# Batch 1 of a retention layer in two-pair blocks with DMA transposes, at the end of the first token tile

## Chip, cores, metric

The kernel runs on one core of a Trainium2 chip. The metric is the time of one execution on the device, in microseconds (us). The kernel before took 535.51 us (median of 4 runs, 535.12 to 537.06; the prediction starts from one of them, 535.76).

The engines are named as the profile names them: PE multiplies matrices, PEld loads its weights, DVE is the vector engine, ACT the scalar engine, POOL the general engine, SP the engine that only starts transfers. DMA queue q1 ("hardware") carries what SP starts, q0 ("software") what POOL starts.

## The reference

```
# retention, batch 8, heads 8, 576 tokens, 64 per head
scores = (1/8) * q @ k.T                       # per batch and head
ret    = (scores * D) @ v                      # D[i,j] = gamma_h ** (i-j) for i >= j, else 0
x      = ret.transpose(0, 2, 1, 3).reshape(4608, 512)
# four experts, mixed by given probabilities
p      = domain_probs / (domain_probs.sum(-1) + 1e-9)
out    = sum over e of p[:, e] * (relu(x @ w1[e]) @ w2[e])     # w1 512x1024, w2 1024x512
```

## The kernel before

Retention is computed in chunks of 128 tokens. The decay is split into factors on q and k, so a chunk needs scores (k against q), a causal mask, key-value products that are summed from chunk to chunk, and values. The 576 tokens of a batch are four chunks and a remainder of 64. The experts run over nine tiles of 512 tokens. In tile 0 ("plain": up and down projections of the four experts, in 32 numbered slots), the retention of batch 1 has to be slipped in between the projections; later batches are slipped into later tiles.

Scores need q and k with the head dimension on partitions, so both are transposed after their cast to bf16. There are two ways to do this. Both are in the class "Unit" (256 tokens of four heads), which serves batches 0 and 1:

```python
        def trans_pe(self, between=0):                      # 8 PE instructions, one ACT copy
            self.qk = atp.tile([128, 2, 2, 2, C], BF16, tag="qkT", name="qkT0")
            pt = ring_tile("pt", [128, 2, 2, 2, 2 * C], BF16)
            for i, n in ((1, "k"), (0, "q")):
                # ...
                        nc.tensor.transpose(pt[:, i, r, g, 0:C], # ... bf of n ...
                                            ident)
            nc.scalar.activation(# ... self.qk <- pt ...
                                 Copy)

        def trans_dma(self):                                # two transfers on SP's queue, no PE
            self.qk = atp.tile([128, 2, 2, 2, C], BF16, tag="qkT", name="qkT1")
            for i, n in ((1, "k"), (0, "q")):
                nc.sync.dma_start_transpose(out=self.qk[:, i].rearrange("p r g t -> p (r g) t"),
                                            in_=self.bf(n).rearrange("p r h d -> p (r h d)"))
```

Batch 1 is four units in tile 0. The first two are transposed on PE, the last two by DMA:

```python
    load_w2(0); load_w1(1); later_tables(); load_w2(1); load_rem(0, nc.gpsimd)   # POOL's queue, q0
    load_w1(2); load_w2(2); load_v(0); load_v(1); load_w1(3); load_v(2); load_w2(3)
    # ...
    def v_cast(u):
        vs[u].cast("k", nc.vector)
        vs[u].cast("q", nc.vector)
        vs[u].cast("v", nc.scalar)
        if u > 1:
            vs[u].trans_dma()
        if u == 0:
            load_v(3)
    # slots of cast, PE transpose, scores and key-values, values
    for u, (c, tr, sc, o) in enumerate(((17, 20, 22, 23), (19, 22, 24, 25), (24, 0, 28, 29), (25, 0, 29, 30))):
        add(c, lambda u=u: v_cast(u))
        if u < 2:
            add(tr, lambda u=u: vs[u].trans_pe())
        add(o, lambda u=u: vs[u].values())
        add(sc, lambda u=u: v_head(u))
```

Batches 2 to 7 use the class "Duo": two pairs of heads over all 512 tokens, in one "block" (values of the block before, key-values, scores), always with DMA transposes on SP's queue:

```python
        def cast(self, p):                    # casts of k, q (and a copy of v), then
            # ...
            for t, n in ((self.kT[p], "k"), (self.qT[p], "q")):
                nc.sync.dma_start_transpose(out=t, in_=bfs[p % 2][n][:, :, :, :].rearrange("p c h d -> p (c h d)"))
```

Of the kernel before, what the change touches and what calls it, by code (L numbers as in the profile page):

```python
# [23 lines left out]
def kernel(  # L24
# [10 lines left out]
    nc = tc.nc  # L35
# [79 lines left out]
    def load_unit(raw, b, hf, g, eng):  # L115
        for n, src in srcs:
            eng.dma_start(out=raw[n],
                          in_=src[b, 4 * g:4 * g + 4, 2 * C * hf:2 * C * hf + 2 * C, :]
                          .rearrange("h (p r) d -> p h (r d)", r=2))

    units0 = ((0, 0), (1, 0), (0, 1), (1, 1))
    p0 = const.tile([128, NT // 128, E], FP32, name="p0")
    prb = tpool.tile([128, N // 128, E], FP32, tag="p1", name="prb")
    for u, (hf, g) in enumerate(units0):
        load_unit({n: raw0[u][n][:, :, :, :].rearrange("p h r d -> p h (r d)") for n in "kqv"}, 0, hf, g, nc.sync)
    nc.sync.dma_start(out=p0, in_=moe_domain_probs[0:NT, :].rearrange("(g p) e -> p g e", p=128))
    nc.sync.dma_start(out=prb, in_=moe_domain_probs.rearrange("(p t) e -> p t e", p=128))
# [103 lines left out]
    class Duo:  # L231
        def __init__(self, b, d):
            self.b, self.d = b, d
            self.ps = slice(2 * d, 2 * d + 2)
            self.qT, self.kT, self.sT = {}, {}, {}

        def cast(self, p):
            for n, eng, g in (("k", nc.gpsimd, gk), ("q", nc.gpsimd, gq)):
                eng.tensor_tensor(bfs[p % 2][n], raw1[n],  # L239
                                  g[:, :, 2 * p:2 * p + 2].unsqueeze(3).to_broadcast([128, NC, 2, D]), op=MULT)  # L240
            nc.gpsimd.tensor_copy(bv[p], raw1["v"])
            self.kT[p] = dpl.tile([128, NC, C], BF16, tag="kT", name="kT", bufs=2)
            self.qT[p] = dpl.tile([128, NC, C], BF16, tag="qT", name="qT", bufs=4)
            for t, n in ((self.kT[p], "k"), (self.qT[p], "q")):
                nc.sync.dma_start_transpose(out=t, in_=bfs[p % 2][n][:, :, :, :].rearrange("p c h d -> p (c h d)"))
# [4 lines left out]
        def kv(self):  # L250
            kvp = ring_tile("kvp", [128, 2, NC, D])
            for i, p in self.pairs():
                for c in range(NC):
                    for j in range(2):
                        nc.tensor.matmul(kvp[64 * j:64 * j + 64, i, c:NC, :], lhsT=bfs[p % 2]["k"][:, c, j, :],
# [19 lines left out]
        def values(self):  # L275
            o = ring_tile("o", [128, 2, SM])
            for i, p in self.pairs():
# [3 lines left out]
            for i, p in self.pairs():  # L281
                for c in range(NC):
                    for j in range(2):
                        nc.tensor.matmul(o[64 * j:64 * j + 64, i, c * C:(c + 1) * C], lhsT=bv[p][:, c, j, :],  # L284
                                         rhs=self.sT[p][:, j, c, :], start=False, stop=(c == NC - 1),
                                         skip_group_check=True)
            n0 = self.b * S
            a = 0
            while a < SM:
                t = (n0 + a) // NT  # L290
                z = min(SM, (t + 1) * NT - n0)
                nc.scalar.activation(xt_of(t)[:, self.ps, n0 + a - t * NT:n0 + z - t * NT], o[:, :, a:z], Copy)  # L292
                a = z

# [58 lines left out]
    def up_group(h, t, e, i):  # L353
        ph = ring_tile("ph", [128, 2, NT])
        x = xt_of(t)
        for f in range(2):
            fc = 2 * i + f
            for dc in range(NDC):
                nc.tensor.matmul(ph[:, f, :], lhsT=w1_sb[e][:, dc, fc * 128:(fc + 1) * 128],  # L359
                                 rhs=x[:, dc, :], start=(dc == 0), stop=(dc == NDC - 1))  # L360
        fk = e * NFC + 2 * i
# [50 lines left out]
    def w_sum(which, lo, hi):  # L412
        sl = slice(lo, hi)
        if which == 3:
            nc.vector.tensor_tensor(t3w[:, sl], wx[1][:, sl, 1], wx[0][:, sl, 1], op=SUB)
        if which == 1:
            nc.vector.tensor_tensor(wx[0][:, sl, 1], wx[0][:, sl, 1], wx[0][:, sl, 0], op=SUB)
        if which == 2:
            nc.vector.tensor_tensor(t2w[:, sl], wx[1][:, sl, 1], wx[0][:, sl, 1], op=SUB)
        if which == 4:  # L420
            nc.vector.tensor_tensor(t4w[:, sl], wx[1][:, sl, 0], t2w[:, sl], op=SUB)
# [88 lines left out]
    class Unit:  # L510
        def __init__(self, b, hf, g, raw, bf, carry=None):
            self.b, self.hf, self.g, self.raw, self.bfs, self.carry = b, hf, g, raw, bf, carry
# [5 lines left out]
        def cast(self, n, engine):  # L518
            dst = self.bf(n).rearrange("p r h d -> p h r d")
            if n == "v":  # L520
                if engine is nc.scalar:
                    nc.scalar.activation(dst, self.raw["v"], Copy)
                else:
                    engine.tensor_copy(dst, self.raw["v"])
# [16 lines left out]

        def trans_dma(self):
            self.qk = atp.tile([128, 2, 2, 2, C], BF16, tag="qkT", name="qkT1")
            for i, n in ((1, "k"), (0, "q")):
                nc.sync.dma_start_transpose(out=self.qk[:, i].rearrange("p r g t -> p (r g) t"),
                                            in_=self.bf(n).rearrange("p r h d -> p (r h d)"))
# [20 lines left out]
        def kv(self):  # L567
# [14 lines left out]
            if hf == 1 and self.carry is None:  # L582
# [7 lines left out]
            for j in range(2):  # L590
                jr = slice(64 * j, 64 * j + 64)
                dst = sbd[jr, gs, 2 * hf:2 * hf + 2, jr]
                src = kvp[jr, :, :, jr]
                if hf == 1 and self.carry is not None:
                    nc.vector.tensor_tensor(dst, src,
                                            self.carry[jr, gs, :].unsqueeze(2).to_broadcast([64, 2, 2, D]), op=ADD)
                else:
                    nc.scalar.activation(dst, src, Copy)
                if hf == 0 and self.carry is not None:
                    nc.vector.tensor_copy(self.carry[jr, gs, :], kvp[jr, :, 1, jr])  # L600

        def values(self):
            self.values_own()
            self.values_carried()
# [12 lines left out]
        def values_carried(self):  # L617
# [9 lines left out]
            n0 = self.b * S + i0  # L627
            for g in range(2):
                p = 2 * self.g + g
                a = 0  # L630
                while a < 2:
                    t = (n0 + C * a) // NT
                    z = 2 if n0 + 2 * C <= (t + 1) * NT else a + 1
                    lo, hi = n0 + C * a - t * NT, n0 + C * z - t * NT
                    w = z - a
                    nat = lambda ap: ap.rearrange("p (a t r) -> p a r t", a=w, r=2)
                    src = lambda x, y: o[:, x:y, g, 0:C].rearrange("p a (r t) -> p a r t", r=2)
                    if hi <= NT:
                        nc.scalar.activation(nat(xt_of(t)[:, p, lo:hi]), src(a, z), Copy)
                    else:  # L640
                        m = (NT - lo) // 2
                        for tt, d0, u0, u1 in ((t, lo, 0, m), (t + 1, 0, m, C // 2)):
                            nc.scalar.activation(
                                xt_of(tt)[:, p, d0:d0 + 2 * (u1 - u0)].rearrange("p (t r) -> p r t", r=2),
                                o[:, a, g, 0:C].rearrange("p (r t) -> p r t", r=2)[:, :, u0:u1], Copy)
                    a = z

    bfv0 = lambda g: {(n, hf): bf0[n][:, hf, g] for n in "kqv" for hf in range(2)}
    us = [Unit(0, hf, g, raw0[u], bfv0(g)) for u, (hf, g) in enumerate(units0)]
# [35 lines left out]
    mixing_weights()  # L685
# [8 lines left out]
    first = ctx.enter_context(ExitStack())  # L694
    fpool = first.enter_context(tc.tile_pool(name="fpool", bufs=1))
    q1 = fpool.tile([128, 2, 2, 4, D], BF16, name="q1")
    raw2 = fpool.tile([128, 3, 2 * NC * D], FP32, name="raw2")
    raw1u = {n: raw1[n][:, :, :, :].rearrange("p c j d -> p (c j d)") for n in "kqv"}
    bf1 = [{}, {}]
    for g in range(2):  # L700
        kv1 = opool.tile([128, 2, 2, 4, D], BF16, tag="o", name=f"kv1_{g}")
        for n in "kqv":
            a = bfs[g][n][:, :, :, :].rearrange("p c j d -> p (c j d)").rearrange("p (r h d) -> p r h d", r=2, h=4)
            bf1[g][n, 0] = a
            bf1[g][n, 1] = q1[:, g] if n == "q" else kv1[:, "kv".index(n)]
    rx = [spool.tile([128, 1024], FP32, tag="S", name=f"rx{i}") for i in range(2)]
    rawxu = {"k": rx[0][:, 0:512], "q": rx[0][:, 512:1024], "v": rx[1][:, 0:512]}
    raws = (raw1u, rawxu, {n: raw2[:, "kqv".index(n), :] for n in "kqv"}, raw1u)
    carry = tpool.tile([128, NP, D], FP32, tag="p1", name="carry")
    vs = [Unit(1, hf, g, {n: raws[2 * hf + g][n].rearrange("p (h r d) -> p h r d", h=4, r=2) for n in "kqv"},  # L710
               bf1[g], carry) for hf in range(2) for g in range(2)]

    def load_v(u):
        load_unit({n: raws[u][n].rearrange("p (h x) -> p h x", h=4) for n in "kqv"}, 1, vs[u].hf, vs[u].g, nc.gpsimd)

    load_w2(0)
    load_w1(1)
    later_tables()
# [4 lines left out]
    load_v(0)  # L723
    load_v(1)
    load_w1(3)
    load_v(2)
    load_w2(3)

    def remainder(slots, b, at):
        add = lambda i, f: slots.setdefault(i, []).append(f)  # L730
        x = Rem(b)
        l, c, tr, s, o = at
        if b > 0:
            add(l, lambda: load_rem(b))
        add(c, lambda: x.cast(nc.vector))
        add(tr, x.trans_pe)
# [137 lines left out]
```

## Time and profile before

| | before |
|---|---|
| time | 535.51 us (4 runs) |
| span of the profiled run | 533.7 us |
| PE | 526.5 us busy, 4260 instructions |
| PE's waits | under 3 us in all |
| granted PE clock | full in every slice |

The lines behind this table are in the prediction below. Two more views follow, the second behind the prediction. The first is the table of stretches. Columns: the stretch, its length, busy time and count of PE, PEld, DVE, ACT and POOL, then the granted PE clock, the mean busy share of a DMA engine, and GB/s. Before:

```profile
60.00:70.00 10.00, 10.00 (x123) 5.16 (x122) 8.19 (x14) 6.20 (x12) 0.00 (x0) 1.00 0.64 150
70.00:80.00 10.00, 9.98 (x102) 4.87 (x101) 5.97 (x10) 3.87 (x11) 0.00 (x0) 1.00 0.55 150
```

The second is the view of the DMA queues from 69 to 75 us, when the kernel before runs its only DMA transposes of tile 0 (queue: packets, MB, share of 16 engines; then transfers with their size or count and the median us from issue to landing):

```profile
q1 hardware_dynamic: 1984, 0.48, 39.9%
...
qkT<-kv SPq DMA_TRANSPOSE x2, 2.5
qkT<-q SPq DMA_TRANSPOSE x2, 3.2
```

No line of q0 stands there: the software queue, with the weights and the loads of batch 1, was empty. These are medians of two: the four transposes landed 2.4 to 4.0 us after their issue under that condition.

### The profile page before, as it was taken

Reading aid. Unit: us, or ns where it says so; the run is one execution under the profiler, and the core shown is the slowest. Engines: PE = TensorE matmul, PEld = TensorE weight load, DVE = VectorE, ACT = ScalarE, POOL = GpSimd, SP = SyncE. Lnnn points to the kernel's source line nnn. Section 1 sums busy time; section 2 is a strip of 40 time slices with the busy share of each in tenths; the row PEclk is TensorE's granted clock in tenths of the full one; section 3 lists DMA queues with packets and bytes.
Section 4 is the critical chain, followed back from the end, with each engine's and each line's share of the span. In section 5 each row is a group of like instructions: output and inputs, shape, how many; then the busy total and the mean of one; then the engine's idle time right before and its main releaser. Section 6 shows DMA issues by size and latency. Waiting matters only on the chain.

```text
span 533.7 us, 10229 instructions
## 1 busy us (share of the span) xinstructions
PE 526.5 (99%) x4260; PEld 342.4 (64%) x4260; DVE 361.7 (68%) x456; ACT 86.0 (16%) x175; POOL 144.5 (27%) x187
## 2 busy tenths in 40 slices
PE   8999999999999999999999999999999999999997
PEld 4644544478745885478646865587548844884486
DVE  6426668895577767697578767777765567557763
ACT  4723450012101121020101001100110000000010
POOL 5734104236235334335132603153000000000000
PEclk9999999999999999999999999999999999999999
DMA  9999947877879967937353655454010111110001
GB/s 240 205 213 250 239 114 190 165 156 168 143 168 166 174 138 145 158 81 167 101 135 95 152 134 112 107 120 124 20 41 21 60 39 41 41 41 20 1 21 60
DMA packets 145118, 63.55 MB, mean 119 GB/s; under 512 B 124240, under 2 KB 135888, under 8 KB 145072
## 3 DMA queue, kind: packets, MB, share of 16 engines
q1 hardware_dynamic: 134752, 43.50, 38.2%
q0 software_dynamic: 10176, 19.27, 16.4%
q8 instruction: 33, 0.54, 0.4%
q10 hardware_dynamic: 144, 0.13, 0.1%
q14 instruction: 13, 0.11, 0.1%
HBM read 53.56 MB, written 9.51 MB: 118 GB/s over the span
## 4 chain that ended last, share of the span: by engine, by line
PE 73%; ACT 2%; DVE 0%; issue 0%
PE ph L359 37%; PE pd L471 34%; ACT xt L292 2%; PE o L284 1%; PE o L279 1%; PE py L471 1%; DVE h L365 0%; PE sr L338 0%; PE or L344 0%; PE or L346 0%; DVE ob L499 0%
## 5 line engine op out<-in xcount | busy, mean ns | idle before, releaser
L359 PE MATMUL ph<-xt,w 128*128 128x512 bf16 x1136 | 251.0, 379 | 0.8 <-DVE h L365 0.2
L365 DVE SCALAR_TENSOR_TENSOR h<-ph,pB 128x1024 bf16<-128x1024 f32 x128 | 156.5, 1224 | 58.7 <-PE ph L359 58.0
L359 PEld LDWEIGHTS <-w 128*128 128x128 bf16 x1136 | 109.9, 98 | 127.9
L471 PEld LDWEIGHTS <-h 128*128 128x128 bf16 x1024 | 100.0, 98 | 13.3
L471 PEld LDWEIGHTS <-s 128*128 128x128 bf16 x768 | 75.0, 98 | 8.7
L471 PE MATMUL pd<-wx,h 128*128 128x256 bf16 x512 | 61.1, 273 | 0.2
L471 PE MATMUL pd<-wx,s 128*128 128x256 bf16 x512 | 61.1, 273 | 0.0
L220 POOL DMA_DIRECT2D pB<-pd x28 | 15.8, 565 | 150.9 <-DVE h L365 131.8
L506 POOL TENSOR_TENSOR ob<-v,p 128x256 f32<-128x256 f32 x15 | 11.3, 755 | 114.0 <-DVE v L503 92.5
L239 POOL TENSOR_TENSOR bf_k<-raw_k,gk 128x512 bf16<-128x512 f32 x24 | 25.8, 1073 | 35.3 <-DMA raw_k<-in_k_dram 17.4
L271 DVE TENSOR_TENSOR sT<-s,tri 128x1024 bf16<-128x1024 f32 x24 | 28.3, 1219 | 6.4 <-PE s L269 6.4
L292 ACT ACTIVATE xt<-o 128x768 bf16<-128x768 f32 (+6 forms) x24 | 13.0, 594 | 116.8 <-PE o L284 116.8
L444 DVE TENSOR_TENSOR s<-s,h 128x1024 bf16<-128x1024 bf16 x32 | 31.2, 1013 | 0.0
L471 PE MATMUL pd<-t4w,h 128*128 128x256 bf16 x256 | 30.6, 273 | 0.0
L394 PE MATMUL po<-wx,h 128*128 128x512 bf16 x128 | 29.1, 379 | 0.1
L471 PE MATMUL pd<-t3w,h 128*128 128x256 bf16 x240 | 28.7, 273 | 0.0
L471 PE MATMUL pd<-t2w,s 128*128 128x256 bf16 x240 | 28.6, 273 | 0.0
L479 ACT ACTIVATE p<-pd 128x256 f32<-128x256 f32 x16 | 6.1, 384 | 138.8 <-PE pd L471 106.2
L239 POOL TENSOR_TENSOR bf_q<-raw_q,gq 128x512 bf16<-128x512 f32 x24 | 26.9, 1120 | 3.3 <-DMA raw_q<-in_q_dram 3.1
L442 DVE TENSOR_TENSOR s<-h 128x1024 bf16<-128x1024 bf16 x32 | 24.8, 816 | 0.0
L448 DVE TENSOR_TENSOR s<-h,s 128x1024 bf16<-128x1024 bf16 x32 | 24.7, 811 | 0.0
L488 DVE TENSOR_TENSOR u<-pd,p 128x256 f32<-128x256 f32 x15 | 6.4, 425 | 22.5 <-PE pd L471 22.5
(158 smaller groups left out, 375.2 us busy)
## 6 DMA issues: line engine op xcount, KB each, us to landing
pB<-pd POOLq DMA_DIRECT2D x28, 256.0 KB, 3.7
raw_k<-in_k_dram SPq DMA_DIRECT2D x48, 128.0 KB, 2.8
raw_q<-in_q_dram SPq DMA_DIRECT2D x48, 128.0 KB, 3.0
raw_v<-in_v_dram SPq DMA_DIRECT2D x48, 128.0 KB, 3.0
wx<-in_moe_w_dram POOLq DMA_DIRECT2D x4, 1024.0 KB, 15.4
out_dram<-oa SPq DMA_DIRECT2D x16, 256.0 KB, 2.2
out_dram<-ob SPq DMA_DIRECT2D x15, 256.0 KB, 2.2
w<-in_moe_w_dram POOLq DMA_DIRECT2D x3, 1024.0 KB, 15.1
```

Source lines behind the costliest of these rows:

```text
L220: eng.dma_start(out=pB[t, e], in_=pd[e:e + 1, t * NT:(t + 1) * NT].to_broadcast([128, NT]))
L239: eng.tensor_tensor(bfs[p % 2][n], raw1[n], g[:, :, 2 * p:2 * p + 2].unsqueeze(3).to_broadcast([128, NC, 2, D]), op=MULT)
L271: nc.vector.tensor_tensor(sT[:, :, :, :].rearrange("p j c t -> p (j c) t"), s[:, :, :, :].rearrange("p j c t -> p (j c) t"), tri[:, :].uns ...
L292: nc.scalar.activation(xt_of(t)[:, self.ps, n0 + a - t * NT:n0 + z - t * NT], o[:, :, a:z], Copy)
L359: nc.tensor.matmul(ph[:, f, :], lhsT=w1_sb[e][:, dc, fc * 128:(fc + 1) * 128], rhs=x[:, dc, :], start=(dc == 0), stop=(dc == NDC - 1))
L365: nc.vector.scalar_tensor_tensor(h[:, fk:fk + 2, :], ph, 0.0, pB[t, e][:, :].unsqueeze(1).to_broadcast([128, 2, NT]), op0=MAX, op1=MULT)
L394: nc.tensor.matmul(po[:, g, :], lhsT=h[:, e * NFC + fc, ns * 128:(ns + 1) * 128], rhs=wx[e // 2][:, (e % 2) * NFC + fc, :, :].rearrange("p ...
L442: nc.vector.tensor_tensor(self.alloc("s1")[:, l], h[:, l, self.b], h[:, r, self.b], op=ADD)
L444: nc.vector.tensor_tensor(self.alloc("s2")[:, l], self.s1[:, l], h[:, l, self.a], op=SUB)
L448: nc.vector.tensor_tensor(self.alloc("s4")[:, l], h[:, r, self.a], self.s2[:, l], op=SUB)
L471: mm = nc.tensor.matmul(dst, lhsT=src[:, kk, tok], rhs=rhs(c), start=(start and c == 0), stop=(c == KH - 1), skip_group_check=True)
L506: nc.gpsimd.tensor_tensor(self.ob[:, HF:Dm], self.v, self.p5, op=ADD)
```

## The change

The intent is to take work off PE in tile 0. Batch 1 becomes two blocks like those of the later batches, with all transposes by DMA, and the remainder of batch 0 is transposed by DMA too. Batch 0's units go in another order (tokens 0 to 255 first), and the probabilities are loaded behind the first down weights. The values v of batch 1 are cast to bf16 by their load. One weight-sum step in four goes from DVE to POOL. Cut to its core:

```diff
-    units0 = ((0, 0), (1, 0), (0, 1), (1, 1))
+    units0 = ((0, 0), (0, 1), (1, 0), (1, 1))
-    nc.sync.dma_start(out=p0, ...)            # and prb
     load_w2(0)
+    nc.gpsimd.dma_start(out=p0, ...)
     load_w1(1)
+    nc.gpsimd.dma_start(out=prb, ...)
     later_tables()
     load_w2(1)
     load_rem(0, nc.gpsimd)
     load_w1(2)
     load_w2(2)
-    load_v(0)
-    load_v(1)
     load_w1(3)
-    load_v(2)
+    load_first(0)                              # pairs of heads, runs of 256 bytes; v cast in the load
+    load_first(1)
     load_w2(3)
+    load_first(2)
 ...
-    remainder(slots, 0, (-1, 13, 15, 16, 17))
-    # ... v_cast, v_head and the slots of the four units
+    for at, f in ((10, lambda: rem0.cast(nc.vector)), (10, rem0.trans_dma), (24, rem0.scores), (25, rem0.values)):
+        add(at, f)
+    add(11, lambda: load_first(3))
+    for p, at in enumerate((21, 23, 27, 28)):
+        add(at, lambda p=p: firsts[p // 2].cast(p, nc.vector))    # with the DMA transposes of pair p
+    add(27, lambda: block(firsts[0], None))
+    add(29, firsts[0].values)
+    add(31, lambda: block(firsts[1], None))
+    add(27, lambda: [load_p(1, e, nc.gpsimd) for e in range(E)])
 ...
-    for j, ats in enumerate(((18, 18, 19, 20), (20, 21, 23, 23), (28, 28, 29, 29), (30, 30, 40, 41))):
+    for j, ats in enumerate(((17, 17, 18, 18), (20, 20, 21, 22), (28, 30, 36, 40), (28, 28, 29, 29))):
+        eng = nc.gpsimd if j == 3 else nc.vector
 ...
+        if t == 1:                             # values of the second block between halves of up groups
+            up_part(1, 0, 0, (0, 1))
+            up_part(1, 0, 1, (0, 1))
+            firsts[1].values(True)
+            up_part(1, 0, 2, (0, 1))
```

## The prediction

> **What bounds the kernel now.** I read first the page's busy shares and its 40 slices, then the view of who waited for whom on the matrix engine (PE), then the timeline of PE, and last the timelines of the engines that feed it.
>
> ```profile
> PE 526.5 (99%) x4260; PEld 342.4 (64%) x4260; DVE 361.7 (68%) x456; ACT 86.0 (16%) x175; POOL 144.5 (27%) x187
> ...
> PE   8999999999999999999999999999999999999997
> ...
> PEclk9999999999999999999999999999999999999999
> DMA  9999947877879967937353655454010111110001
> ```
>
> PE is busy 526.5 of 533.7 us, in every slice, at full clock. So time falls only if PE instructions go, and it rises if the new order makes PE wait. The waits of PE are these, in total:
>
> ```profile
> PE w L138 <- DVE zz L131: 1.3, 1, 1.3
> PE s L560 <- ACT qkT L539: 0.5, 2, 0.3
> PE o L623 <- ACT sbd L598: 0.5, 2, 0.2
> PE pt L537 <- DVE bf_q L526: 0.2, 1, 0.2
> PE o L623 <- DVE sbd L595: 0.2, 1, 0.2
> PE ph L359 <- DVE h L365: 0.2, 1, 0.2
> ```
>
> Columns: total us, times, longest. Under 3 us, half of it before the first instruction. There is no stall for the change to remove; the prize must be PE work. The PE timeline has both forms of it side by side: batch 1 as four small "units" inside tile 0 (lines 537, 560, 578, 613, 623), and batch 2 already as two-pair blocks (lines 255, 269, 279, 284):
>
> ```profile
> 56.20 0.39 PE L537 MATMUL pt<-ident,bf_k 128*128 128x128 bf16 x4
> 56.42 0.39 PE L537 MATMUL pt<-ident,bf_q 128*128 128x128 bf16 x4
> 56.64 3.62 PE L394 MATMUL po<-wx,h 128*128 128x512 bf16 x16
> 60.19 0.42 PE L560 MATMUL s<-qkT 64*64 64x128 bf16 x16
> 60.54 0.72 PE L578 MATMUL kvp<-bf_v,bf_k 128*128 128x128 bf16 x8
> 61.19 0.40 PE L537 MATMUL pt<-ident,bf_k 128*128 128x128 bf16 x4
> ...
> 125.32 0.50 PE L279 MATMUL o<-qT,sbd 128*128 128x128 bf16 x6
> 125.75 0.64 PE L284 MATMUL o<-sT,bf_v 128*64 128x128 bf16 x16
> 126.22 0.72 PE L255 MATMUL kvp<-v,bf_k 128*64 128x256 bf16 x16
> 126.88 0.62 PE L269 MATMUL s<-qT,kT 64*128 64x128 bf16 x16
> 127.62 1.91 PE L471 MATMUL pd<-wx,h 128*128 128x256 bf16 x16
> ```
>
> First number: start; second: duration with the pipeline's tail. What a piece costs PE is the distance from its start to the next piece's start: 60.19 to 61.19 is 1.00 us for one unit's scores and key-value products.
>
> **What the Trainium skill says.** "TensorE: Matmul & The Clock Gate", part 1, section "Wait — 56ns, not 53.3ns?", gives 215.7 ns from start to start for 512 columns at the warm clock. The trace agrees: 16 matmuls of 128x512 between 22.27 and 25.7 us are 3.45 us, 216 ns each; the 379 ns of the groups is a latency that overlaps. "SBUF — State Buffer", section "Who interferes with whom", says that a VectorE (DVE) instruction with two SBUF inputs contends with a GpSimd (POOL) instruction that reads SBUF, the second waiting for the first's end. The trace agrees: a weight sum on DVE takes 0.69 us as a rule, and 2.16 us at 100.80 us, while POOL multiplies at 100.80 to 101.86. "DMA: Bandwidth & Descriptors", Specifications, gives 512 B as the least transfer for line rate. The trace agrees in kind: batch 1's second unit landed about 2.1 us after its first (0.75 MB in 512-byte runs), while the remainder's 0.38 MB in 256-byte runs took some 1.9 us of the same queue. "GPSIMD Engine Reference", section "Instruction dispatch", gives about 2.5 cycles per element for two inputs on POOL; 512 elements in 1.04 us are 2.4 cycles at that page's 1.2 GHz.
>
> **The change, part by part.**
>
> Removed from PE, start to start from the timeline: the remainder's transposes 0.54 (46.66 to 47.20); two units' transposes 0.44 + 0.46; four units' scores and key-value products 1.00 + 1.01 + 1.00 + 1.09; four units' values 0.47 + 0.47 + 0.68 + 0.94. Sum 8.10 us, 196 instructions.
>
> Added to PE: two blocks. Batch 2's blocks stand 1.45, 1.40 and 1.39 us for key-values and scores, and 0.90 and 1.00 us for values. Two blocks cost 2 x (1.40 + 0.95) = 4.70 us, 108 instructions. The built programs confirm the count: 88 matmuls fewer. **PE saves 8.10 - 4.70 = 3.40 us.**
>
> Batch 0's order: the same instructions, the 12-product key-value step moved from the second unit to the third. The end of that stage hangs on the fourth unit: its queries are awaited for 0.2 us by DVE at 13.5 us, then follow transpose, copy, scores, mask and values to about 20.6 us, where the second half of the up projection can begin. Order does not move the fourth load, so I count 0, plus or minus 0.3. The first half's tokens are ready earlier, but nobody waited for them.
>
> Probabilities: two loads leave the front of the first queue and go behind the first down weights, which landed at about 26.0 us (POOL, which waits for them, resumes at 26.09) against PE's first use at 25.95. The 16 matmuls before it need 3.45 us and have 3.68. So some 0.2 us is lost there now; an earlier landing saves at most that. **-0.2 us.**
>
> Loads of batch 1: four pairs in 256-byte runs, in place of four units in 512-byte runs. My estimate from the two rates above is 3.6 us a pair in place of 2.3, hence the last pair lands some 5 us later: the DMA share falls to 0.05 at 66 us now, so at about 71 then. Weights gain: the last up weights go ahead of batch 1, and the last down weights wait behind 1.5 MB and not 2.25. They are needed 4.4 us sooner (about 68 us, as this much of the removed work lies before), so this is even.
>
> The end of tile 0 is where a new wait can arise. Call T0 the end of the first block, about 69.5 us (now the last up group of tile 0 ends at 72.53; less 4.4, plus 1.4). Pair 2's transposes may start when the first block's scores have read the two key buffers. The queue's own timeline shows 1.2 to 1.3 us per transpose issued, and 2.5 to 2.9 us to landing. DVE has in a row: two masks (2.35 us for a pair at 109.51), the two casts of pair 3 (0.69 each), a weight sum, two evictions (1.41), another sum, two evictions, two masks. Pair 3's casts thus end at T0 + 3.8, its transposes land at T0 + 7.5. PE reaches the second block after four down groups (1.73 each) and one values step: T0 + 7.9. Without disturbance it just fits. Then the score buffer waits for the eviction (about T0 + 7.3), the first split up group for the second (T0 + 9.9 against T0 + 9.3), and the split up groups (1.73 us) cover the two masks. So 0.5 us of stall at best.
>
> POOL disturbs it: four weight sums of 1024 elements, about 2.1 us each at the 2.4 cycles, are in program order right behind the last loads, so they run from about 71 to 79 us, beside DVE's casts and sums with two SBUF inputs. If two or three of those wait about 1 us each, the second block starts 1 to 3 us late, part of which the slack eats. **My central stall is 1.3 us.** The remainder of batch 1 is similar: its loads sit behind the first output in the queue, transposes land at about 90, and PE wants them at 90.8. I count 0 to 1 us, inside the stall.
>
> Later tiles keep their instructions, and just shift. Sum: -3.4 - 0.2 + 1.3 = -2.3 us, on 535.76: **533.4 us.**
>
> **Rivals.** (1) The tail of tile 0 becomes a wait: loads, casts, transposes and masks no longer keep up, and PE stands 4 us or more; the time is 535.5 to 537. For it: pair 3 has no slack in my count, DVE is 9.1 of 10 us busy at 80 to 90 now, and the POOL contention hits just there. Against it: four groups of independent matmuls and the split up groups were put there to cover. (2) Full hiding: POOL's sums fall in gaps, the transposes come in time, and everything counted on PE is won, also a few tenths in the first 26 us: 531.5 to 532.2. For it: PE has had every other wait hidden so far. (3) The loads: if DMA runs in 256-byte pieces cost more than I estimate, the last down weights come after 69.5 us and pair 3 after 74, and PE loses 2 to 5 us: 535 to 538. Against it: the DMA share shows a valley after 66 us that takes up 5 us.
>
> **Range and chances.** The saving on PE is counted and certain to perhaps 0.3 us; the stall is 0.3 to 5 us. That gives 531.4 to 536.2, with the middle nearer the low end. A gain of 2% would need 10.7 us, three times all the PE work removed; a loss of 2% would need a stall of 14 us. Faster 0.02, within 2% 0.96, slower 0.02.
>
> **What would show each step.** PE at 4172 instructions and about 3.4 us less busy; the two new blocks at 1.4 and 0.95 us. In the PE waits a new row for the second block (scores behind DVE or a transpose) or for values behind the mask, together 1 to 2 us between 65 and 95 us. On POOL four sums of about 2.1 us near 71 to 79 us; on DVE casts or sums above 0.69 us in the same stretch. The last pair lands at 70 to 73 us. The first down group starts about 3.5 us after the up group before it. A PE wait over 3 us, at the last down weights or the second block, proves me wrong; so would a start stage that moved by over 0.5 us.

## The result and the profile after

The changed kernel took **544.04 us** (median of 4 runs, 541.57 to 544.64) against 535.51 us. The ratio is 1.0145, with a 95% interval of 1.0107 to 1.0183: 1.4% slower, inside the 2% band, and 7.8 us above the upper end of my range. Ratios here and below are the mean time of one kernel's runs over that of the other's of the same rounds, so they are not quite the ratio of the medians quoted.

The page of the changed kernel, busy totals and the 40 slices of 13.5 us:

```profile
PE 524.8 (97%) x4172; PEld 341.0 (63%) x4172; DVE 359.0 (66%) x444; ACT 80.7 (15%) x157; POOL 167.4 (31%) x209
...
PE   8999929999999999999999999999999999999997
...
PEclk9999979999999999999999999999999999999999
DMA  9999998768667768556546593534110111010001
```

The 88 instructions are gone, but slice 6 (67.7 to 81.3 us) has PE at 2 tenths and its clock at 7. The DMA row says that this slice is the last of a long stretch of nearly full DMA engines (six slices at 9). PE's waits have a new first line, and its timeline shows the place (start, duration, instruction, in brackets the idle time just before and what ended it):

```profile
PE s L269 <- DMA qT<-bf_q: 9.8, 2, 6.3
```

```profile
67.73 0.75 PE L255 MATMUL kvp<-bf_v,bf_k 128*64 128x256 bf16 x16
71.98 0.40 PE L269 MATMUL s<-qT,kT 64*128 64x128 bf16 x8 [3.50 <-DMA qT<-bf_q]
78.70 0.61 PE L269 MATMUL s<-qT,kT 64*128 64x128 bf16 x8 [6.32 <-DMA qT<-bf_q]
79.25 5.70 PE L414 MATMUL po<-wx,h 128*128 128x512 bf16 x16
...
85.79 3.63 PE L414 MATMUL po<-wx,h 128*128 128x512 bf16 x16
```

The scores of the first block waited for the transposed queries of pair 0 (3.50 us) and then of pair 1 (6.32 us). Two equal groups of 16 down-projection matmuls follow: the first took 5.70 us, the second 3.63 us. The stretches show why (columns as before):

```profile
60.00:70.00 10.00, 8.48 (x63) 4.12 (x61) 3.87 (x7) 5.44 (x7) 6.23 (x9) 1.00 1.34 108
70.00:80.00 10.00, 1.70 (x18) 0.91 (x19) 3.17 (x4) 0.00 (x0) 4.60 (x7) 0.66 1.33 184
```

The granted clock (third from last) has a mean of 0.66 over the second stretch. That is a mixture. Cut at the places where it changes, the stretches read:

```profile
69.00:73.20 4.20, 0.40 (x8) 0.25 (x8) 0.00 (x0) 0.93 (x2) 0.00 (x0) 1.00 1.05 153
73.30:83.40 10.10, 4.70 (x18) 1.87 (x19) 6.57 (x7) 0.00 (x0) 7.93 (x10) 0.50 1.43 196
83.50:90.00 6.50, 6.50 (x61) 3.47 (x59) 3.35 (x5) 1.08 (x2) 6.26 (x4) 1.00 0.89 241
```

PE was busy for 0.40 of 4.20 us, and then the clock was half for about 10 us, in which the first group ran.

The sum closes. Waits 3.50 + 6.32 = 9.8 us, slow matmuls 5.70 - 3.63 = 2.1 us, less the 3.4 us that the change saves on PE: +8.5 us. The spans differ by 541.9 - 533.7 = 8.2 us.

Next, why the transposes came so late. SP's timeline shows their issue:

```profile
59.15 1.19 SPq L245 DMA_TRANSPOSE kT<-bf_k  x1
60.43 1.23 SPq L245 DMA_TRANSPOSE qT<-bf_q  x1
62.99 1.67 SPq L245 DMA_TRANSPOSE kT<-bf_k  x1
64.76 2.21 SPq L245 DMA_TRANSPOSE qT<-bf_q  x1
```

The queries of pair 0 were issued at 60.43 and released PE at 71.98; those of pair 1 went out at 64.76 and released it at 78.70. The casts and the issue were in time; from issue to the release of PE it took 11.6 and 13.9 us, where the kernel before shows about 3 to landing. The DMA view gives the medians over 58 to 68 us, and the queues' packets over 71 to 76 us:

```profile
kT<-bf_k SPq DMA_TRANSPOSE x2, 8.9
qT<-bf_q SPq DMA_TRANSPOSE x2, 12.6
```

Each line is a median of two. One by one, the keys and queries of pair 0 landed 3.5 and 11.4 us after issue, those of pair 1 14.3 and 13.8.

```profile
q0 software_dynamic: 736, 0.77, 88.9%
q1 hardware_dynamic: 746, 0.18, 41.1%
```

The two queues had almost the same number of packets through in those 5 us. A transpose of 128 x 512 bf16 elements is 131,072 bytes, and 0.18 MB in 746 packets is about 240 bytes each, so one transpose is some 512 packets of 256 bytes (worked out from these lines). The software queue's packets were about 1 KB each. If the DMA engines serve the queues in turn, packet by packet, each small packet of a transpose waits for a large packet of a load. The Trainium skill has such turns: "DMA: Bandwidth & Descriptors", section "Queues, rings and completion order", says that each DMA engine goes round the queue rows it has work for, and drains one whole packet before it moves on. Its packet is a bundle of several descriptors (single pieces of a transfer); no run here shows that this is what the profile counts as a packet. The equal counts agree with turns, one for one. I had not drawn on the page in the prediction.

The fast one of the four fits too. From 60 to 62 us, when the keys of pair 0 were on their way, the packets of the software queue were small themselves, about 140 bytes:

```profile
q0 software_dynamic: 1054, 0.15, 134.3%
q1 hardware_dynamic: 538, 0.13, 33.1%
```

So small packets beside small ones got through in 3.5 us.

The equal counts hold from 67 to 77 us, but for 69 to 70 us (27 and 18, when both nearly stood): single microseconds read 139 and 135, 151 and 147, 107 and 108, 211 and 215. They do not hold everywhere. From 62 to 67 us both queues crawled, the hardware queue more (6 to 47 packets in a microsecond, the software queue 59 to 95). Taking turns is thus not the whole of it, and this crawl stays unexplained.

The remainder's transposes met the same fate earlier: issued at 37.93 and 39.46, landed 11.6 and 12.1 us later, with 625 and 624 packets in the two queues from 40 to 46 us. Nobody waited for them, but in that stretch, by the same reading, they took turns from the weights.

### The profile page after: what moved, and what is told of

Same layout as the page of the kernel before. It is cut to its first block, busy times and chain, and to the rows that moved or that the text cites. A ratio compares the mean times of both kernels' runs of the same rounds, so it can differ in the third digit from the quotient of the medians. Undisturbed runs are those within 1.5% of the kernel's fastest.

```text
span 541.9 us, 10073 instructions
## 1 busy us (share of the span) xinstructions
PE 524.8 (97%) x4172; PEld 341.0 (63%) x4172; DVE 359.0 (66%) x444; ACT 80.7 (15%) x157; POOL 167.4 (31%) x209
## 4 chain that ended last, share of the span: by engine, by line
PE 72%; ACT 2%; DVE 0%; issue 0%
PE ph L375 36%; PE pd L491 33%; ACT xt L302 2%; PE o L285 1%; PE o L280 1%; PE py L491 1%; DVE h L385 0%; PE or L356 0%; PE sr L350 0%; PE or L358 0%; PE s L269 0%; PE kvp L255 0%; DVE ob L519 0%
## 5 line engine op out<-in xcount | busy, mean ns | idle before, releaser
L491 PEld LDWEIGHTS <-h 128*128 128x128 bf16 x1024 | 100.0, 98 | 13.3
L218 POOL DMA_DIRECT2D pB<-pd x32 | 17.9, 566 | 155.6 <-DVE h L385 148.7
L271 DVE TENSOR_TENSOR sT<-s,tri 128x1024 bf16<-128x1024 f32 x28 | 33.0, 1218 | 6.7 <-PE s L269 6.7
L302 ACT ACTIVATE xt<-o 128x768 bf16<-128x768 f32 (+8 forms) x30 | 15.3, 567 | 134.9 <-PE o L285 134.9
L414 PE MATMUL po<-wx,h 128*128 128x512 bf16 x128 | 30.5, 399 | 0.0
L414 PEld LDWEIGHTS <-h 128*128 128x128 bf16 x128 | 12.6, 102 | 16.7 <-issue 2.9
```

The costliest lines, as they stand in the source:

```text
L218: eng.dma_start(out=pB[t, e], in_=pd[e:e + 1, t * NT:(t + 1) * NT].to_broadcast([128, NT]))
L271: nc.vector.tensor_tensor(sT[:, :, :, :].rearrange("p j c t -> p (j c) t"), s[:, :, :, :].rearrange("p j c t -> p (j c) t"), tri[:, :].uns ...
L302: done.append(nc.scalar.activation(xt_of(t)[:, 2 * self.d + i:2 * self.d + z2, n0 + a - t * NT:n0 + z - t * NT], o[:, i:z2, a:z], Copy))
L414: nc.tensor.matmul(po[:, g, :], lhsT=h[:, e * NFC + fc, ns * 128:(ns + 1) * 128], rhs=wx[e // 2][:, (e % 2) * NFC + fc, :, :].rearrange("p ...
L491: mm = nc.tensor.matmul(dst, lhsT=src[:, kk, tok], rhs=rhs(c), start=(start and c == 0), stop=(c == KH - 1), skip_group_check=True)
```

## The experiments

The theory: **a DMA transpose issued while the software queue is busy with large packets can land 9 to 18 us after its issue, and not 2.5 to 3; the first block's scores wait for it, and the clock falls during the wait.** (Not each one does: besides the 3.5 us above, those of pairs 2 and 3 in the changed kernel landed after 4.6 to 5.5 us beside a busy queue.) In the texts, A is this theory. Its rivals, where named, are the slower loads, the POOL sums beside DVE, and the other parts of the change (order, probabilities). Each kernel was timed over 3 rounds (the two so marked over 5), with the kernel before on the same chip. All outputs are right.

| run | made from | median us | ratio to before [95%] |
|---|---|---|---|
| before_units_dma | before | 544.03 | 1.0146 [1.0125, 1.0168] |
| before_front | before | 535.21 | 0.9992 [0.9972, 1.0012] |
| after_pairs_pe | after | 537.56 | 1.0029 [1.0006, 1.0051] |
| after_rem_pe | after | 541.46 | 1.0100 [1.0081, 1.0119] |
| after_both_pe | after | 538.35 | 1.0035 [1.0008, 1.0062] |
| after_dve_sums | after | 542.02 | 1.0125 [1.0106, 1.0144] |
| pairs_pe_late_p | after | 539.76 | 1.0085 [1.0035, 1.0134] |
| pairs_pe_dve | after | 538.84 | 1.0058 [1.0036, 1.0080] |
| all_pairs_pe | after | 535.42 | 0.9984 [0.9939, 1.0030] |
| all_pairs_pe_dve (5 rounds) | after | 534.82 | 0.9982 [0.9966, 0.9998] |
| all_pe_dve (5 rounds) | after | 533.93 | 0.9976 [0.9961, 0.9992] |
| after_filled | after | 546.91 | 1.0202 [1.0164, 1.0241] |
| before_idle_transposes | before | 536.81 | 1.0019 [0.9999, 1.0040] |
| before_idle_copies | before | 535.95 | 1.0007 [0.9991, 1.0022] |

### One part of the change alone, in the kernel before

**DMA transposes for the first two units.** Loads, order, blocks and sums stay as before.

```diff
-        if u > 1:
-            vs[u].trans_dma()
+        vs[u].trans_dma()
 ...
-        if u < 2:
-            add(tr, lambda u=u: vs[u].trans_pe())
```

> The kernel before with one thing changed: the first two units of batch 1 get their transposes from the DMA queue (as units 3 and 4 already do) at the moment of their casts, 50 to 54 us, while the software queue still loads weights. Theory A (transposes issued beside the software queue's loads crawl, packet by packet in turn with them): the four transposes land 9 to 14 us after issue and not 2.5, PE waits 1 to 5 us in all at the scores of these units, the last down weights land later; PE saves 0.9 us; time 536 to 540. Theory B (the loads of batch 1 in 256-byte runs and with a cast in the DMA are what is slow; here they stay in 512-byte runs): the transposes land in 2.5 to 4 us, no new PE wait, time 534.6.

It took 544.03 us, the same loss as the whole change, from this part alone. The loss is larger than the text expected; the direction is A's, and nothing else of the change is needed for it. PE's waits:

```profile
PE s L560 <- DMA qkT<-bf_q: 4.5, 1, 4.5
```

The four transposes landed 10.6, 12.4, 16.8 and 14.9 us after issue. The clock fell here too (a mean of 0.68 from 60 to 66 us).

**The front alone**: batch 0's order and the later probabilities (cut; the steps that work out the mixing weights move to other slots with them).

```diff
-    units0 = ((0, 0), (1, 0), (0, 1), (1, 1))
+    units0 = ((0, 0), (0, 1), (1, 0), (1, 1))
-    (loads of p0 and prb on nc.sync)
     load_w2(0)
+    nc.gpsimd.dma_start(out=p0, ...)
     load_w1(1)
+    nc.gpsimd.dma_start(out=prb, ...)
```

> The kernel before with only the two small parts of the change: batch 0's units in the new order and the probabilities behind the first down weights (batch 1 and all transposes as before). My reckoning: nothing waits on either, 0 to 0.3 us of gain; time 535.2 to 535.8, no PE wait above 0.5 us that the kernel before does not have. If one of these parts were the cause of the loss, 537 or more.

535.21 us: no effect on the time, as expected.

### Transposes back on PE, in the changed kernel

**Pairs 0 and 1** (the first block):

```diff
+            if self.b == 1 and p in PE_PAIRS:     # PE_PAIRS = (0, 1)
+                return                            # no DMA transposes
...
+        def trans_pe(self, p):                    # 8 transposes on PE, two ACT copies
+    for p, at in zip(PE_PAIRS, (23, 25)):
+        add(at, lambda p=p: firsts[p // 2].trans_pe(p))
```

> The changed kernel with pairs 0 and 1 of batch 1 transposed on PE (16 transposes, some 0.9 us) and not by DMA; loads untouched. Theory A: the two waits of 3.5 and 6.3 us at the first block's scores go, the last down weights and pair 2 land some 5 us sooner, the clock stays at 1.00; a rest of 0 to 3 us may stay at the second block; time 533 to 537. Theory B: the last down weights and pair 2 still land at about 75 us, PE waits at the first down group instead, 4 us or more; time 539 or more.

537.56 us: 6.5 us of the 8.5 us loss came back. The wait at the first block is gone, and one at the second block is left:

```profile
PE s L281 <- DMA qT<-kq: 2.4, 1, 2.4
```

This is pair 3. In this run its transposes went out at 75.67 and 76.97 us, beside the loads of tile 1's probabilities, and were late as well.

**The remainder alone**:

```diff
-    ... (10, rem0.trans_dma), ...
+    ... (14, rem0.trans_pe), ...
```

> The changed kernel with only the remainder's two transposes (issued at 38 us) put back on PE. Theory A: its two DMA transposes no longer take turns with the weight loads of 38 to 52 us, so the third down weights land about 2 us sooner and the two waits at the first block's scores fall from 9.8 to about 7 to 9 us; time 541 to 543.5. Theory B: no transposes matter, time 544 plus the 0.5 us of PE work.

541.46 us. The wait at the first block fell from 9.8 to 5.8 us, probably because the loads that share the DMA engines with the block's transposes were further along; I did not trace this. The fall is larger than the text expected (to 7 to 9 us). The rest of the wait stayed, so the remainder is a smaller part of the loss.

**Both together**:

> The changed kernel with the remainder and pairs 0 and 1 transposed on PE; pairs 2 and 3 stay with DMA, after the loads. Theory A: no PE wait over 2 us between 60 and 95 us; PE work 3.4 - 0.9 - 0.5 = 2.0 us below the kernel before; time 532.5 to 535.5, so it is the candidate to beat both. Theory B: 539 or more, as the loads stay.

538.35 us, a miss: 3 us more than expected, and no better than the pairs alone. Pair 3's wait was 3.1 us here, and the mean clock was 0.68 and 0.64 from 80 to 90 us. I had treated the waits as a sum of independent parts; taking one away uncovered the next.

**All four pairs on PE** (slots 23, 25, 29, 30):

> The changed kernel with all four pairs of batch 1 transposed on PE (32 transposes, 1.8 us); only the remainder stays with DMA. Theory A: no PE wait for a transpose at all; PE work is 3.4 - 1.8 = 1.6 us under the kernel before; time 533.5 to 535, which would beat both kernels. Rival C (late loads and casts of pair 3): a PE wait of 1 to 3 us stays, at the transposes of pair 3; time 535.5 to 538.

The four runs took 537.17, 533.67, 537.94 and 533.50 us. The granted clock of the core was 0.997, 1.000, 0.997 and 1.000 in the same order. Two runs lie in the expected range and two above it, 4 us longer and with a lower clock. In the profiled one (at 0.997) the longest waits near the second block were 0.6 and 1.2 us, both behind DVE. They lie in a stretch in which PE was busy less than half of the time, and half clock follows:

```profile
79.30:82.70 3.40, 1.66 (x34) 1.26 (x33) 3.40 (x6) 1.18 (x2) 3.32 (x2) 1.00 0.51 179
82.80:86.10 3.30, 3.06 (x7) 1.13 (x8) 2.22 (x2) 0.00 (x0) 3.22 (x3) 0.50 0.47 108
```

By my estimate from these lines, 3.4 us at half clock cost at most 1.7 of the 4 us; the waits behind DVE are the rest as far as I can see.

### The other suspects

**The POOL sums alone**, back to DVE in the changed kernel:

```diff
-    ... (28, 28, 29, 29))):
-        eng = nc.gpsimd if j == 3 else nc.vector
+    ... (33, 35, 38, 42))):
+        eng = nc.vector
```

> The changed kernel with only POOL's four sums put back on DVE, all transposes as changed. Theory A (transposes beside loads are the main loss): the two waits of 3.5 and 6.3 us stay, 541.5 to 544.5, as the sums come after them. If the contention of POOL and DVE were the main loss, as my prediction had it: 537 or less.

542.02 us, and PE's wait for the queries was still 7.8 us. The median is 2 us lower, but the intervals of the two kernels overlap, so what the sums on POOL cost here is 2 us or less, if anything.

**Probabilities of tile 1 later** (slot 27 to 30, pairs 0 and 1 on PE), to give pair 3's transposes a quiet queue:

```diff
-    add(27, lambda: [load_p(1, e, nc.gpsimd) for e in range(E)])
+    add(30, lambda: [load_p(1, e, nc.gpsimd) for e in range(E)])
```

> The kernel with pairs 0 and 1 on PE (537.6), and the four loads of tile 1's probabilities moved from ahead of POOL's weight sums to behind them, so that the transposes of pair 3 (issued at about 76 us) have no software queue traffic beside them. Theory A: they land 2.5 to 3.5 us after issue and not 5.8; the PE wait of 2.4 us at the second block's scores falls under 1 us, the clock stays at 1.00; time 533.8 to 536. Rival C (pair 3's casts are simply late, or DVE is): the wait stays at 2 us or more, time 537 or more.

On the transposes the theory held: pair 3's landed 2.4 and 2.5 us after issue. On the time it missed: 539.76 us. POOL's sums now began at 72.3 us, behind no load, and ran beside DVE's casts. PE waited 3.1 and 1.5 us for DVE. The two casts of pair 3 took 1.77 and 2.61 us:

```profile
74.92 2.61 DVE L240 TENSOR_TENSOR kq<-rawr_q,gq 128x512 bf16<-128x512 f32 x1
```

Against 0.69 us as a rule, this is the contention of DVE and POOL that the prediction feared. In the changed kernel itself these sums ran later, from 81 to 91 us, behind late loads, where they did less harm.

**Pairs 0 and 1 on PE, sums on DVE**:

> Pairs 0 and 1 on PE, pairs 2 and 3 by DMA, sums on DVE. Pair 3's transposes still run beside the software queue (last loads and the probabilities of tile 1), so they land 5 to 6 us after issue; the PE wait at the second block stays 1 to 2.5 us; time 534.5 to 537.

538.84 us, above the expected range. The wait for pair 3 was 3.3 us, where 1 to 2.5 were expected (its transposes landed 6.9 and 6.1 us after issue, not 5 to 6); a wait of 2.1 us for the last down weights was not foreseen.

**All pairs on PE, sums on DVE**, without and with the remainder on PE as well:

> All four pairs of batch 1 on PE, and the last four weight sums back from POOL to DVE, spread over tile 1 (DVE has 0.5 us free behind each eviction there). Theory: the weight sum of 2.6 us at 76 us on DVE was held up by POOL's sums; at 0.7 us the evictions behind it come 2 us sooner, the PE waits of 0.6 and 1.2 us at the second block go, the clock stays at 1.00 in every run; time 533.4 to 534.2 in all runs, which beats both kernels. If POOL's sums are not what delayed DVE: waits and the split into runs of 533.6 and 537.6 us stay.

> The same with the remainder on PE too: 0.5 us more on PE, the weights about 1.5 us sooner, so PE and DVE wait less for pair 2 (some 0.5 us); 533.4 to 534.4, equal to the other within noise.

534.82 and **533.93 us**. The first missed its text: all runs were to take 533.4 to 534.2 us at full clock, and they took 533.41 to 535.93 (four of six above), though the clock was full (0.999 or 1.000). The second has its median in the expected range, two of six runs above. It has no DMA transpose in tile 0's busy stretch at all, and is faster than both kernels, though by little: 0.9976 [0.9961, 0.9992] of the time before, the interval below 1. All its runs had a clock of 0.999 or 1.000. Its stretch from 70 to 80 us, to set beside the two shown above:

```profile
70.00:80.00 10.00, 9.89 (x103) 5.72 (x102) 7.14 (x10) 4.63 (x9) 4.08 (x7) 1.00 0.85 217
```

PE is full again and the DMA engines moved 217 GB/s, against 184 in the changed kernel.

### The clock

**Idle matmuls in the waits of the changed kernel** (16 after the key-values, 29 before pair 1's scores), to hold the clock up:

```diff
+                if self is firsts[0] and i == 1:
+                    fill(29)
...
+            if new is firsts[0]:
+                fill(16)
```

> The changed kernel with 45 idle matmuls (their result is not used) in the two waits at the first block's scores, some 9.7 us of them, so that PE never pauses there. Theory: the waits stay the same length in time but the clock stays at 1.00 and the 16 matmuls behind them take 3.5 us and not 5.6; so about 2 us of the loss are the clock's; time 541.5 to 542.5. If the clock costs nothing: 544.

546.91 us, inconclusive. The waits there shrank to 2.6 us, but the transposes had landed before most of the second filler (27 matmuls, 7.3 us) ran, so the filler itself held PE up. The group behind the filler took 3.63 us and not 5.70, and half clock lasted only from 77.5 to 80.8 us. That the clock falls because PE stands is therefore argued from the order in time, and from the two groups of 5.70 and 3.63 us, but not isolated.

The other runs add to the argument. Ten of the profiled runs show a fall of the clock in this part of the kernel, always to 0.50, for stretches of about 3.4 to 10 us, and always right after some 3.4 us in which PE was busy for 0.40 to 1.66 us. The six without such a stretch there (before, before_front, the two idle runs below, all_pairs_pe_dve, all_pe_dve) have full clock throughout. But one case speaks against a plain rule by busy time: with the filler, PE was busy for only 1.45 us from 26.2 to 29.6 us, and the clock stayed at 1.00.

### Taking turns, by itself

Two kernels add four transfers on SP's queue to the kernel before, at 50 to 54 us, from the first two units' q and k, into places that nobody reads. One uses transposes, the other plain copies cut into 256-byte pieces, so each has the same 512 packets. PE waits for neither.

```diff
+        if u < 2:
+            for i, n in enumerate("kq"):
+                nc.sync.dma_start_transpose(out=(t4w, t3w)[u][:, 12 + 2 * i:14 + 2 * i, :]...,   # or dma_start
+                                            in_=vs[u].bf(n)...)
```

> The kernel before, unchanged in all its work, plus four DMA transposes of the first two units' keys and queries at 50 to 54 us into places that nobody reads; PE still does the real ones. Turn-taking (A): they land 9 to 17 us after issue, though nothing else in the kernel changed, and slow the loads beside them, so the last down weights land 2 to 6 us later; PE, which waits for none of the four, loses only what the weights' delay costs: 0 to 4 us, time 535.5 to 540. If the transposes were late only for what the changed schedule does to them: 2.5 to 4 us to landing and no change in time.

> The same with four plain copies of the same tiles, in 256-byte pieces, so the same 512 packets each in the same hardware queue at the same time. If a packet of the hardware queue takes its turn with one of the software queue whatever it is: the copies land late too, 7 to 14 us, but the loads need not suffer; time 535.5 to 538. If the transpose itself is what does not go along with other traffic: the copies land in 3 to 5 us and nothing slows; time 535.5.

The transposes landed 10.3, 13.5, 18.2 and 14.9 us after issue, the copies 10.4, 13.1, 15.5 and 16.4. Packets of the two queues from 58 to 62 us, first with the transposes, then with the copies:

```profile
q0 software_dynamic: 464, 0.62, 89.9%
q1 hardware_dynamic: 466, 0.11, 36.4%
```

```profile
q0 software_dynamic: 565, 0.73, 91.2%
q1 hardware_dynamic: 570, 0.14, 26.0%
```

The counts are equal in both (in each microsecond from 56 to 64 us too), and both kinds are about equally late. So the lateness belongs to the transfers of 512 small packets beside a busy queue, not to transposes as such. That it is the number of packets, and not any transfer on SP's queue, is read from the equal counts and not isolated; copies in larger pieces would have tested it, and were not run. Nor are turns all of it: the first packet of the first transpose moved some 4 us after its issue at 51.84 us, and the later transfers stood behind the earlier ones of their own queue.

There is one difference: in these 4 us all queues together moved 182 GB/s with transposes and 217 with copies, against 225 in the kernel before, and from 62 to 66 us 174 and 237 against 253. These totals have the added transfers in them. The software queue alone moved 0.62 MB with transposes, 0.73 with copies and 0.88 in the kernel before, and then 0.55, 0.79 and 1.01 MB. So both slow the neighbouring loads, transposes more. The time shows little of it, 536.81 and 535.95 us, as PE waited only 1.6 and 0.4 us for the last down weights. Why transposes slow the loads more is open.

## Why the prediction was wrong

**PE's saving: right.** 88 matmuls fewer, as counted. The values of the first block stand at 1.0 us, start to start, and the key-values and scores of the second at 1.3 us (predicted 0.95 and 1.40). The version without these waits gives about 4 x 0.45 + 0.54 = 2.3 us of the saving back to PE transposes, which leaves 1.1 us, and its span of 532.2 us is 1.5 us below that of before.

**Batch 0's order and the probabilities: right.** The front alone did not move the time. In the changed kernel the first down group started 3.45 us after the up group before it, as foreseen, so the 0.2 us is there but too small to show in the time.

**The loads of batch 1: right for the block that stalled, wrong in size.** Pairs 0 and 1 were cast at 58.4 and 62.3 us without waiting for their loads. The last down weights, which I had called even, landed at 75.0 us against 65.7 before; with all transposes on PE (all_pe_dve) at 67.8, so about 7 of these 9 us go with the transposes. The end of batch 1's loads, which I had put 5 us later, moved from 67.9 to 83.0 us, and still to 74.9 with all transposes on PE: 7 us without them. So the shorter runs and the new order were put too low as well.

**The step that failed** is in the paragraph on the end of tile 0: "The queue's own timeline shows 1.2 to 1.3 us per transpose issued, and 2.5 to 2.9 us to landing." Those figures are medians of the transposes of later tiles, where the software queue moved 80 packets or fewer beside each, and I used them for pair 3 as if it came after the loads. The first two pairs I did not work through, though they run beside the loads (DMA share 1.34 from 60 to 70 us). Measured, their transposes took 11.6 and 13.9 us to release PE, and PE stood 9.8 us. That the transposes are the cause was shown twice: put alone into the kernel before, they cost as much as the whole change (544.03 us), and with all of them on PE (and the sums on DVE) the changed kernel takes 533.93 us. The kernel before had kept the first two units on PE and only the last two on DMA. The same sentence failed again for pair 3 once pairs 0 and 1 were put right (6.4 and 5.7 us to landing).

**A term that was missing**: the clock. The sum had no entry for a lower clock after a stall; it measured 2.1 us. And the range did not follow from its own parts: 535.76 - 3.6, with a stall of 0.3 to 5 us and 0.3 us either way, gives 532.2 to 537.5, not 531.4 to 536.2. The result lies outside both.

**The POOL disturbance: mechanism right, place wrong.** The sums took 2.37, 2.45, 2.62 and 2.13 us (2.1 foreseen), but ran from 81 to 91 us in place of 71 to 79, behind a queue that was late itself. Where they did meet the casts, in the run with the later probabilities, they cost DVE what was feared and more.

**The rivals.** The first (the tail becomes a wait of 4 us or more) came nearest in effect, but it put the wait at pair 3, for want of DVE time. The stall was at pairs 0 and 1, for want of DMA turns. The signs of the third (loads) came true, the last down weights after 69.5 us (75.0) and pair 3 after 74 (its cast at 80.5), and the time did not stay within its 535 to 538; most of the weights' delay came from the transposes, and PE's stall at the first block probably hid the rest. None of the listed signs named the first block.

**Luck.** "Within 2%" came true because the band is wide: a gain of 0.4% was forecast, and a loss of 1.4% measured.

What stays open: why the two queues crawl from 62 to 67 us, below any even share; why transposes slow loads more than copies of the same packets; whether copies in larger pieces would be in time; and what exactly makes the clock fall (a sparse stretch of 3.4 us came before each fall, but one such stretch had none).

## What to carry to other kernels

Take the landing time of a transfer from a stretch with the same traffic as where it is to run: a figure from an idle queue said 3 us here, and the busy queue gave up to 18. A transfer of hundreds of small packets beside long loads pays, as these counts read, a turn for each packet, so under load a few PE instructions (0.45 us a pair, in gaps that PE has to fill anyway) can be cheaper than a "free" DMA transpose. When an engine's stall is taken away, look at once for the next one behind it, and count the clock as part of a stall's price.

## What the Trainium skill lacked or had wrong

- "DMA: Bandwidth & Descriptors", section "Queues, rings and completion order": the turns between queues are stated, and the equal counts agree (736 and 746; 464 and 466; 565 and 570). What they mean for a transfer of small packets is not there: about 512 packets of 256 bytes landed 10 to 18 us after issue beside loads in packets of about 1 KB, and 2.4 to 4.0 us alone. Nor is it said whether the page's packet is the one that a profile counts.
- No page that I read says that DMA transposes slow the loads beside them, and more than plain copies do: from 58 to 62 us the software queue moved 0.62 MB beside transposes, 0.73 beside copies in the same number of packets, and 0.88 with neither. The equal counts do not hold in every microsecond either (62 to 67 us of the changed kernel).
- "TensorE: Matmul & The Clock Gate", section "What's actually happening": the table gives half the clock after at least one idle window of about 3.4 us. The half agrees: 0.50 in each fall here, for about 3.4 to 10 us. But no window had to be idle: the clock fell after 3.4 us in which PE was busy for 1.66 us (all four pairs on PE, waits of 0.6 and 1.2 us) and 1.02 us (pairs 0 and 1 on PE), and did not after 3.4 us with 1.45 busy (the run with the filler). The page gives no figure for how busy a window must be.
